# Window attention with a Sinkhorn mixture of experts on one core: the order of filler products, of the first weights' preparation and of two small copies

## Chip, cores and metric

The kernel runs on one core of one Trainium2 chip. The metric is the device time of one execution in microseconds (us), from the first to the last instruction and a little around it. Four compute engines and the DMA queues each work through their own list of instructions in order, and wait for each other by semaphores: TensorE (PE; its weight loads are PEld), VectorE (DVE), ScalarE (ACT), GpSimd (POOL), and SyncE (SP), from which all DMAs of this kernel are issued.

## What is computed

Attention over a window of 64 positions, for 4 batches of 8 heads, 576 positions and 64 columns a head, then a mixture of 8 experts over the 2304 x 512 result:

```python
def _attn_ref(q, k, v):
    scores = scale * np.matmul(q, k.transpose(0, 1, 3, 2))
    mask = (rel >= 0) & (rel < window)
    scores = np.where(mask, scores, -1000000000.0)
    scores = scores - np.max(scores, axis=-1, keepdims=True)
    attn = np.exp(scores)
    attn = attn / (np.sum(attn, axis=-1, keepdims=True) + 1e-09)
    return np.matmul(attn, v).astype(np.float32)

def _moe_ref(x, w_gate, w1, w2):
    logits = x @ w_gate
    P = np.exp(logits - logits.max())
    for _ in range(8):
        P /= P.sum(1, keepdims=True) + 1e-09
        P /= P.sum(0, keepdims=True) + 1e-09
        P *= N / E
    for e in range(E):
        out += P[:, e:e + 1] * (np.maximum(x @ w1[e], 0.0) @ w2[e])
    return out
```

with q, k, v of (4, 8, 576, 64), w_gate (512, 8), w1 (8, 512, 1024), w2 (8, 1024, 512), all float32.

## The kernel before

The 2304 rows are 18 tiles of 128. All products of the experts are made from values split in a high and a low part (three products in place of one). The program's order is written out by hand: each engine executes its instructions in the order in which the code emits them.

**Stage 1** (0 to 184 us of the trace) is the attention, a loop over steps s = 0 to 18 (the tiles, and one more). A full step emits, in this order: SP loads k and q of tile s + 2 (`load_kq`), v and the shifted v; PE makes the score products of tile s (`products`), DVE adds the mask and takes the maximum (`masked`); in even steps the gate product of an earlier pair of tiles (`gate`, ACT copies it out); PE transposes k and q of tile s + 1 (`transposes`; DVE evacuates k to kT, ACT q to qT, POOL copies the overlap of kT); ACT makes the exponentials of the first half (`exps`), DVE masks the second half; then a first `do_fill`; then PE transposes the first half of tile s - 1's weights (`attn_T`; ACT copies them to aT), DVE and POOL normalise the first half of tile s (`normalise`), PE transposes the second half of tile s - 1; ACT makes the exponentials of the second half; then a second `do_fill`; in even steps `gate_T`; then the values of tile s - 1 (`values`: PE, then the xs or xc cast and the xr copy on ACT with a DVE subtraction between them); then the second half of tile s is normalised, its DVE sum behind the subtraction of `values`. So attn_T of a step waits for normalises of the step before it, and the DVE work of each step's end comes after the values.

**Fillers.** For the six pairs of tiles that the first MoE pass does not take, the first 512 columns of expert 0 are worked out within the attention: four `mm1_s` (12 matmuls of 256 columns) and two `mm2_s` (12 of 512, whose result ACT copies and SP stores) for each pair. They wait in the list `fill`; `do_fill(n)` adds n to a credit and starts what the credit pays for, an mm1 at 0.5 and an mm2 at 1. `SHARE` gives 1 and 0.5 to the two places of steps 3 to 6 and 9 to 12, and 0.5 and 0.5 to the others. That deals: three mm1 in step 3; mm1 and mm2 in 4; mm2 and mm1 in 5; three mm1 in 6; nothing ahead of attn_T and one mm2 behind it in 7 and 8; the same again in 9 to 14; an mm1 at both places in 15 and 16; nothing ahead and an mm2 behind in 17 and 18; the last pair's six after the loop.

**Weights within stage 1.** `fetch_s` loads w1 and w2 of the fillers in two halves each; `warm_weights` splits the next half (`split_s`: ACT casts, POOL subtracts), in steps 1, 2 and twice in step 3, in step 3 once before and once behind the second `do_fill`. The first pass's weights follow: `fetch1(0)` (SP) and `sums1(0)` (four POOL operations) at the end of step 14, `split1(0)` (three ACT casts, three POOL subtractions), `fetch1(1)` and `fetch2(0)` at the end of step 15, `sums1(1)` at the end of step 17. The ring `stg` has two buffers in this stage, so `fetch2(0)` reuses the one that `split1(0)` reads. At the end of steps 6, 12 and 16 POOL also sums a pair of x (`x_sums`), whose casts (ACT) and subtractions (POOL) follow through the list `later`, one at each of two places in a step.

**First MoE pass** (184 to about 700 us). 16 units u of two weight groups each: 14 products by `Group.run`, then six `mm2(u, t)`, 12 matmuls of 512 columns each into one of two y banks. In unit 0 (expert 0, first columns) ACT copies y to acc; later units add on DVE. Between the mm2 stand Sinkhorn's steps, one at t = 0, 2, 4 (`step()` takes the next of `pending`: seven times column and row, a last column, then `prob_rows(1)` and `prob_rows(2)`), so the last column step falls in unit 2 at t = 2, `prob_rows(1)` at t = 4, `prob_rows(2)` in unit 3 at t = 0. `prob_rows` copies six rows' probabilities to `own` in three DVE copies, transposes that on PE, and stores it. DVE's sums of w2 (`sum_step`) stand between the mm2 as well, and POOL prepares the next weights.

**Second and third pass** (to the end) are not touched.

Of the kernel before, what the change touches and what calls it, by code (L numbers as in the profile page):

```python
# [8 lines left out]
F32 = mybir.dt.float32  # L9
# [12 lines left out]
def window_attention_sinkhorn_moe(ctx: ExitStack, tc: tile.TileContext, q, k, v, w_gate, w1, w2, out):  # L22
    nc = tc.nc
    B, H, S, D = q.shape
    NT, DM = out.shape
    E, _, FF = w1.shape
    P = 128
    WIN = 64
    T = NT // P
# [3 lines left out]
    ITERS = 8  # L33
    TP = 6
    NPASS = T // TP
    PAIRS = [[2, 5, 7], [1, 4, 8], [0, 3, 6]]
# [19 lines left out]
    prob = const.tile([P, T + 1, E + 1], F32, name="prob")  # L56
# [70 lines left out]
    def fetch1(i):  # L127
        if i < len(groups):
            e, c = groups[i]
            stg = r_stg.new()  # L130
            nc.sync.dma_start(out=stg, in_=w1[e, :, c * 2 * P:(c + 1) * 2 * P].rearrange("(k p) f -> p k f", p=P))
            raw1[i] = stg
# [141 lines left out]
    def mm2(u, t):  # L274
        i0 = 2 * u
        e, c = groups[i0]
        yp = ps["y"]()
        o, n = divmod(t, 2)
        o *= P
        i = 0  # L280
        for gi in (i0, i0 + 1):
            for f in range(2):
                g, w = gt_[gi, f, n], wt2[gi, f]
                for a, x in ((0, 0), (0, 1), (1, 0)):
                    nc.tensor.matmul(yp, lhsT=g[:, a, o:o + P], rhs=w[:, x, :], start=(i == 0), stop=(i == 11))  # L285
                    i += 1
        at = acc[:, t, :]
        tt = TILES[0][t]
        pr = prob[:, tt, e:e + 1]
        first = c == 0  # L290
        if e == 0:
            if first:
                nc.scalar.copy(out=at, in_=yp)  # L293
            else:
                nc.vector.tensor_tensor(out=at, in0=yp, in1=at, op=ALU.add)
        elif e == 1:

            a1 = side["acc"][:, t, :]
            if first:
                nc.scalar.copy(out=a1, in_=yp)  # L300
            else:
                nc.vector.tensor_tensor(out=a1, in0=yp, in1=a1, op=ALU.add)
        else:
            if first and e == 2:
                nc.scalar.activation(out=at, in_=at, func=AF.Copy, scale=prob[:, tt, 0:1])
                nc.vector.scalar_tensor_tensor(out=at, in0=side["acc"][:, t, :], scalar=prob[:, tt, 1:2], in1=at, op0=ALU.mult, op1=ALU.add)
            nc.vector.scalar_tensor_tensor(out=at, in0=yp, scalar=pr, in1=at, op0=ALU.mult, op1=ALU.add)  # L307
# [27 lines left out]
    with tc.manual_schedule():  # L335
        with ExitStack() as p1:
# [268 lines left out]

            fill = []

            credit = [0.0]
            SHARE = {s: (1, 0.5) if s < 15 and s % 6 in (3, 4, 5, 0) else (0.5, 0.5) for s in range(3, T + 1)}

            def do_fill(n):
                credit[0] += n
                while fill and credit[0] >= fill[0][0]:
                    cost, f = fill.pop(0)
                    f()
                    credit[0] -= cost

            new_kT(0)
            nc.vector.memset(kT[0][:, :, 0:WIN], 0.0)
# [6 lines left out]
            def warm_weights(s):  # L626
                if first and s > 0:
                    split_s(first[0][0], first[0][1], held.pop(0))
                    first.pop(0)
# [10 lines left out]
            for s in range(T + 1):  # L640
                if s + 2 < T and s != 3:
                    load_kq(s + 2)
                if s == 1:
                    held.append(fetch_s("w1", 2))
                if s < T:
                    load_vs(s)
                if s + 1 < T:
                    load_v(s + 1)
                if s == 3:
                    x_parts(0)  # L650
                if s == 0:
                    held.append(fetch_s("w1", 0))
                if s == 1:
                    nc.sync.dma_start(out=wg[:, :, 0:E], in_=w_gate.rearrange("(k p) e -> p k e", p=P))
                if s == 2:
                    held.append(fetch_s("w2", 0))
                    load_kq(5)
                    held.append(fetch_s("w2", 2))
                joint = 2 <= s < T
                ahead = s in (1, 2)  # L660
                if s < T:
                    products(s, (0, 1) if joint else (0,))
                    masked(s, 0)
                if s >= 4 and s % 2 == 0:
                    gate((s - 4) // 2)
                if s < 2:
                    keep_clock(4 if s else 0)
                if s == 3:
                    keep_clock(4, ps["h"]()[:, :P])
                    do_fill(SHARE[s][0])  # L670
                if s + 1 < T:
                    transposes(s + 1)
                if s == 1:
                    keep_clock(2)
                if s < T and not ahead:
                    exps(s, 0)
                if joint:
                    masked(s, 1)
                if later:
                    later.pop(0)()  # L680
                if s > 3:
                    do_fill(SHARE[s][0])
                if 0 <= s - 1 < T:
                    attn_T(s - 1, 0)
                if s < 2:
                    products(s, (1,))
                    masked(s, 1)
                if ahead:
                    if s == 2:
                        keep_clock(11, ps["h"]()[:, :P])  # L690
                    attn_T(s - 1, 1)
                    exps(s, 0)
                if s < T:
                    normalise(s, 0)
                if s == 0:
                    keep_clock(4)
                if 0 <= s - 1 < T and not ahead:
                    attn_T(s - 1, 1)
                if s > 2:
                    warm_weights(s)  # L700
                if s == 2:
                    values(1, lambda: exps(2, 1))
                elif s < T:
                    exps(s, 1)
                if later:
                    later.pop(0)()
                if s > 2:
                    do_fill(SHARE[s][1])
                if s == 3:
                    warm_weights(s)  # L710
                if s >= 4 and s % 2 == 0:
                    gate_T((s - 4) // 2)
                if s == 1:
                    keep_clock(4)
                if 0 <= s - 1 < T:
                    if s != 2:
                        values(s - 1)
                    raw.pop(("v", s - 2), None)
                if s < T:
                    normalise(s, 1)  # L720
                if s < 3:
                    warm_weights(s)
                if s >= 2 and s % 2 == 0:
                    j = s // 2 - 1
                    if j:
                        x_parts(j)
                    if PASS[2 * j][0]:
                        for c in range(4):
                            fill.append((0.5, lambda c=c, j=j: mm1_s(j, c)))
                        for t in (2 * j, 2 * j + 1):  # L730
                            fill.append((1, lambda t=t: mm2_s(t)))
                if s == T - 4:
                    fetch1(0)
                    sums1(0)
                if s == T - 3:
                    split1(0)
                    fetch1(1)
                    fetch2(0)
                if s == T - 1:
                    sums1(1)  # L740

            do_fill(0.5)
            gate(T // 2 - 1)
            do_fill(1)
            gate_T(T // 2 - 1)
            nc.vector.tensor_reduce(out=max1, in_=logit, axis=AX.XY, op=ALU.max)
            do_fill(1)
# [62 lines left out]
        with ExitStack() as p2:  # L810
# [12 lines left out]
            pending = []  # L823
# [24 lines left out]
            def sk_col():  # L848
# [4 lines left out]
                nc.vector.reciprocal(out=c, in_=c)  # L853
                nc.vector.tensor_tensor(out=pv, in0=pv, in1=c[:, None, :].to_broadcast([P, T, E]), op=ALU.mult)

            def prob_rows(p):
                n = TP * (E + 1)
                rp = sk_tile([n, P], "rp")
                own = sk_p.tile([P, TP, E + 1], F32, tag="own", name="own", bufs=1)
                for i, j in enumerate(PAIRS[p]):  # L860
                    nc.vector.tensor_copy(out=own[:, 2 * i:2 * i + 2, :], in_=prob[:, 2 * j:2 * j + 2, :])
                nc.tensor.transpose(rp, own.rearrange("p t e -> p (t e)"), ident)
                row = sk_p.tile([n, P], F32, tag="row", name="row")
                nc.scalar.copy(out=row, in_=rp)
                nc.sync.dma_start(out=prow[p], in_=row)

            sk_exp()
            sk_row()
            pending += [lambda: (sk_col(), sk_row())] * (ITERS - 1) + [sk_col] + [lambda p=p: prob_rows(p) for p in prow]

            for _ in range(2):
                nc.tensor.matmul(ps["b"](), lhsT=xc[0][:, 0, 0, 0:P], rhs=xc[0][:, 0, 0, :], start=True, stop=True)
# [629 lines left out]
```

## Time and profile before

| | us |
|---|---|
| median of 3 runs (lowest to highest) | 1588.26 (1586.72 to 1590.82) |
| the profiled execution, its own time | 1586.67 |
| its span, first to last instruction | 1584.9 |
| PE busy | 1553.6 (98%) |
| POOL busy | 1011.2 (64%) |
| DVE busy | 972.4 (61%) |
| ACT busy | 770.0 (49%) |

The span falls in stage 1 (184 us), the first pass (to about 700 us) and the two others. An engine's busy time leaves out what it waits. The chain of waits follows the work that ended last back from the end: at each step to what released it, or to the instruction before it on its engine; it tells which engine's time is the kernel's time. A view of a stretch gives for each engine its busy time and, in brackets, its instructions; PEclk is the clock granted to TensorE as a share of 2.4 GHz.

### The profile page before, as it was taken

The numbers are of one execution on the slowest core, as the hardware profiler recorded it, in microseconds if no ns is written. First come the engines' busy times: TensorE is split into PE (matmuls) and PEld (weight loads), VectorE is DVE, ScalarE is ACT, GpSimd is POOL, SyncE is SP. The second block draws the span as 40 slices with busy tenths as digits, with TensorE's granted clock in tenths as the row PEclk, the third lists the DMA queues.
The fourth block names the chain that finished last, engine by engine and source line by source line (L and its number), as shares of the span: only waits on it lengthen the run. The fifth ranks groups of instructions, "written<-read, shape, count | busy, mean of one in ns | idle before, by whom it ended". The sixth has DMA issues, their size and how long they took to land.

```text
span 1584.9 us, 27121 instructions
## 1 busy us (share of the span) xinstructions
PE 1553.6 (98%) x9643; PEld 1477.5 (93%) x9643; DVE 972.4 (61%) x1803; ACT 770.0 (49%) x1692; POOL 1011.2 (64%) x943
## 2 busy tenths in 40 slices
PE   8998989899999999999999999999999999999998
PEld 7786778789989988999999999999999999999998
DVE  6778257555554555555667566566656566576576
ACT  6667443444433443346455555445465454454453
POOL 6436376656785787526766766656676656657665
PEclk9999999999999999999999999999999999999999
DMA  9786355647676766697577676565885565665652
GB/s 214 176 187 156 114 199 208 211 174 259 226 285 225 260 207 243 227 328 243 184 227 239 200 249 203 189 213 177 296 305 184 183 220 177 192 221 172 198 168 100
DMA packets 235989, 334.39 MB, mean 211 GB/s; under 512 B 70818, under 2 KB 150286, under 8 KB 231886
## 3 DMA queue, kind: packets, MB, share of 16 engines
q1 hardware_dynamic: 235854, 332.66, 65.3%
q8 instruction: 76, 1.25, 0.3%
q14 instruction: 59, 0.48, 0.1%
HBM read 238.57 MB, written 90.63 MB: 208 GB/s over the span
## 4 chain that ended last, share of the span: by engine, by line
PE 93%; DVE 3%; ACT 1%; POOL 1%; DMA 1%; issue 1%; SPq 0%; ACTq 0%; POOLq 0%; DVEq 0%
PE qb L226 18%; PE y L285 15%; PE qa L226 12%; PE qc L226 12%; PE qb L1213 12%; PE qa L1213 8%; PE qc L1213 8%; PE yp L600 2%; PE hp L586 2%; PE vp L496 1%; PE tp L481 1%; DMA acc<-in_moe_w_dram 1%; PE sp L427 1%; PE tp L407 0%; DVE nm L453 0%
## 5 line engine op out<-in xcount | busy, mean ns | idle before, releaser
L226 PE MATMUL qb<-xc,w1c 128*128 128x384 f32 x1656 | 328.4, 336 | 0.0
L1100 POOL TENSOR_TENSOR G<-sm,G 128x384 fp32r<-128x384 f32 x176 | 179.0, 1017 | 195.7 <-ACT G L1096 195.7
L226 PEld LDWEIGHTS qb<-xc,w1c 128*128 128x128 f32 x1656 | 291.2, 188 | 0.7 <-ACT qb L1114 0.3
L285 PE MATMUL y<-w2c,g 128*128 128x512 f32 x1152 | 271.4, 394 | 4.5 <-ACT acc L293 4.1
L285 PEld LDWEIGHTS y<-w2c,g 128*128 128x128 f32 x1152 | 217.1, 190 | 51.1 <-ACT acc L293 4.5
L226 PE MATMUL qa<-xc,w1c 128*128 128x384 f32 x1104 | 218.2, 337 | 0.0
L226 PE MATMUL qc<-xc,w1c 128*128 128x384 f32 x1104 | 217.8, 336 | 0.0
L226 PEld LDWEIGHTS qa<-xc,w1c 128*128 128x128 f32 x1104 | 194.6, 188 | 1.2
L226 PEld LDWEIGHTS qc<-xc,w1c 128*128 128x128 f32 x1104 | 194.4, 188 | 0.0
L1221 DVE TENSOR_TENSOR acc<-qb,acc 128x384 f32<-128x384 f32 x171 | 95.0, 555 | 123.3 <-PE qb L1213 110.7
L185 POOL TENSOR_TENSOR w2c<-stg,w2c 128x512 fp32r<-128x512 f32 x64 | 89.8, 1423 | 114.5 <-PE qb L226 107.9
L794 POOL TENSOR_TENSOR w2c<-wr,w2c 128x512 fp32r<-128x512 f32 x99 | 126.5, 1297 | 34.5 <-ACT w2c L793 30.8
L794 POOL TENSOR_TENSOR wp<-wr,wp 128x512 fp32r<-128x512 f32 x100 | 127.8, 1297 | 27.5 <-ACT wp L793 22.6
L1096 ACT CAST G<-sm 128x384 fp32r<-128x384 f32 x180 | 92.3, 514 | 64.3 <-DVE sm L1107 64.3
L1213 PE MATMUL qb<-G,w2c 128*128 128x384 f32 x552 | 111.2, 336 | 0.0
L1213 PE MATMUL qb<-G,wp 128*128 128x384 f32 x528 | 106.2, 336 | 0.0
L307 DVE SCALAR_TENSOR_TENSOR acc<-y,prob,acc 128x512 f32<-128x512 f32 x72 | 54.0, 750 | 74.1 <-PE y L285 73.5
L1213 PEld LDWEIGHTS qb<-G,w2c 128*128 128x128 f32 x552 | 97.7, 188 | 0.0
L1213 PEld LDWEIGHTS qb<-G,wp 128*128 128x128 f32 x528 | 93.4, 188 | 0.0
L1221 DVE TENSOR_TENSOR acc<-qc,acc 128x384 f32<-128x384 f32 x116 | 64.3, 555 | 41.6 <-PE qc L1213 41.1
L171 POOL TENSOR_TENSOR w1c<-ws,w1c 128x1024 fp32r<-128x1024 f32 x32 | 80.4, 2512 | 0.0
L1107 POOL TENSOR_TENSOR r<-sm,r 128x384 f32<-128x384 f32 x60 | 61.0, 1017 | 30.0 <-DVE sm L1107 22.1
(217 smaller groups left out, 2850.1 us busy)
## 6 DMA issues: line engine op xcount, KB each, us to landing
w1c<-w1d SPq DMA_DIRECT2D x300, 256.0 KB, 4.4
w1d<-w1c SPq DMA_DIRECT2D x30, 1792.0 KB, 7.6
stg<-in_moe_w_dram SPq DMA_DIRECT2D x68, 512.0 KB, 4.0
w1c<-w1d SPq DMA_DIRECT2D x60, 512.0 KB, 4.8
wr<-w2d SPq DMA_DIRECT2D x114, 256.0 KB, 3.5
wr<-in_moe_w_dram SPq DMA_DIRECT2D x85, 256.0 KB, 3.9
w2d<-tf SPq DMA_DIRECT2D x30, 512.0 KB, 4.7
vs<-v SPq DMA_DIRECT2D x35, 128.0 KB, 4.3
```

The lines of the kernel that those rows point to most:

```text
L171: nc.gpsimd.tensor_tensor(out=w[:, sl, 1], in0=src.rearrange("p (s k) f -> p s k f", k=2), in1=f32(w[:, sl, 0]), op=ALU.subtract)
L185: nc.gpsimd.tensor_tensor(out=w[:, 1], in0=src[:, j], in1=f32(w[:, 0]), op=ALU.subtract)
L226: nc.tensor.matmul(bank, lhsT=w[:, ws, a, kk, :], rhs=xc[xs][:, b, kk, :], start=(first and j == 0), stop=(j == 5), skip_group_check=not f ...
L285: nc.tensor.matmul(yp, lhsT=g[:, a, o:o + P], rhs=w[:, x, :], start=(i == 0), stop=(i == 11))
L307: nc.vector.scalar_tensor_tensor(out=at, in0=yp, scalar=pr, in1=at, op0=ALU.mult, op1=ALU.add)
L586: nc.tensor.matmul(hp, lhsT=w1s[c][:, a, kk, :], rhs=xs[j][:, b, kk, :], start=(i == 0), stop=(i == 3 * KD - 1))
L794: nc.gpsimd.tensor_tensor(out=t[:, :, 1, :], in0=r, in1=f32(t[:, :, 0, :]), op=ALU.subtract)
L1096: nc.scalar.copy(out=self.g[:, k, 0, :], in_=src)
L1100: eng.tensor_tensor(out=self.g[:, k, 1, :], in0=src, in1=f32(self.g[:, k, 0, :]), op=ALU.subtract)
L1107: eng.tensor_tensor(out=dst, in0=x, in1=y, op=op)
L1213: nc.tensor.matmul(bank, lhsT=W[p, u, wp][:, g, y, cols], rhs=G7[p, 2 * u + g][:, gp, x, :], start=(start and j == 0), stop=(j == 5), skip ...
L1221: nc.vector.tensor_tensor(out=at, in0=src, in1=at, op=ALU.add)
```

## The change

- In unit 0 the copy of y to acc goes from ACT to DVE.
- `do_fill(n)` takes n fillers, whatever they cost: one ahead of attn_T from step 3 on, one behind it in steps 3 to 16, none behind it in 17 and 18. That deals two mm1 to steps 3, 4, 6, 7, 9, 10, 12, 13, 15 and 16, two mm2 to steps 5, 8, 11 and 14, and one mm2 ahead of attn_T to 17 and 18; after the loop the order is as before.
- The second call of `warm_weights` in step 3 is gone; the last half (w2) is split by the call in step 4, ahead of the second `do_fill`.
- `fetch1(0)` goes from the end of step 14 to that of 7, `sums1(0)` from 14 to 8, `split1(0)` with `fetch1(1)` and `fetch2(0)` from 15 to 11, `sums1(1)` from 17 to 14.
- The three DVE copies to `own` for each of passes 1 and 2 are made right after the last column step, into two buffers; `prob_rows` only transposes, copies and stores.

```diff
         if e == 0:
             if first:
-                nc.scalar.copy(out=at, in_=yp)
+                nc.vector.tensor_copy(out=at, in_=yp)
...
-            credit = [0.0]
-            SHARE = {s: (1, 0.5) if s < 15 and s % 6 in (3, 4, 5, 0) else (0.5, 0.5) for s in range(3, T + 1)}
-
             def do_fill(n):
-                credit[0] += n
-                while fill and credit[0] >= fill[0][0]:
-                    cost, f = fill.pop(0)
+                for f in fill[:n]:
                     f()
-                    credit[0] -= cost
+                del fill[:n]
...
                 if s == 3:
                     keep_clock(4, ps["h"]()[:, :P])
-                    do_fill(SHARE[s][0])
+                    do_fill(1)
...
                 if s > 3:
-                    do_fill(SHARE[s][0])
+                    do_fill(1)
...
-                if s > 2:
-                    do_fill(SHARE[s][1])
-                if s == 3:
-                    warm_weights(s)
+                if 2 < s < T - 1:
+                    do_fill(1)
...
-                            fill.append((0.5, lambda c=c, j=j: mm1_s(j, c)))
+                            fill.append(lambda c=c, j=j: mm1_s(j, c))
                         for t in (2 * j, 2 * j + 1):
-                            fill.append((1, lambda t=t: mm2_s(t)))
-                if s == T - 4:
+                            fill.append(lambda t=t: mm2_s(t))
+                if s == 7:
                     fetch1(0)
+                if s == 8:
                     sums1(0)
-                if s == T - 3:
+                if s == 11:
                     split1(0)
                     fetch1(1)
                     fetch2(0)
-                if s == T - 1:
+                if s == 14:
                     sums1(1)
 
-            do_fill(0.5)
+            do_fill(1)
             gate(T // 2 - 1)
-            do_fill(1)
+            do_fill(2)
...
+            own_rows = {}
+
+            def gather(p):
+                own_rows[p] = own = sk_p.tile([P, TP, E + 1], F32, tag="own", name="own")
+                for i, j in enumerate(PAIRS[p]):
+                    nc.vector.tensor_copy(out=own[:, 2 * i:2 * i + 2, :], in_=prob[:, 2 * j:2 * j + 2, :])
+
             def prob_rows(p):
...
-                own = sk_p.tile([P, TP, E + 1], F32, tag="own", name="own", bufs=1)
-                for i, j in enumerate(PAIRS[p]):
-                    nc.vector.tensor_copy(out=own[:, 2 * i:2 * i + 2, :], in_=prob[:, 2 * j:2 * j + 2, :])
+                own = own_rows.pop(p)
...
-            pending += [lambda: (sk_col(), sk_row())] * (ITERS - 1) + [sk_col] + [lambda p=p: prob_rows(p) for p in prow]
+            pending += [lambda: (sk_col(), sk_row())] * (ITERS - 1) + [lambda: (sk_col(), [gather(p) for p in prow])] + [lambda p=p: prob_rows(p) for p in prow]
```

## Rows read from the trace of the kernel before

**Rows 1.** The page's part 4: chain that ended last, share of the span by engine.
```profile
PE 93%; DVE 3%; ACT 1%; POOL 1%; DMA 1%; issue 1%; SPq 0%; ACTq 0%; POOLq 0%; DVEq 0%
```

**Rows 2.** Waits of PE, 0 to 184 us: for whom, us in total, times, longest.
```profile
PE tp L481 <- POOL s L475: 8.2, 4, 2.9
```

**Rows 3.** Waits of PE, 184 us to the end.
```profile
PE qc L862 <- DVE own L861: 4.2, 2, 3.6
PE y L285 <- ACT acc L293: 4.1, 1, 4.1
```

**Rows 4.** Busy time by stretch, columns as headed; steps 4, 7, 9, 12, 15, 16.
```profile
core 0: us, PE busy (x) PEld busy (x) DVE busy (x) ACT busy (x) POOL busy (x), PEclk, DMA share, GB/s
33.73:47.32 13.59, 10.80 (x119) 8.75 (x115) 6.80 (x15) 8.14 (x22) 7.78 (x8) 0.87 0.71 159
64.61:73.01 8.40, 7.15 (x96) 5.72 (x92) 6.02 (x12) 6.43 (x19) 5.71 (x7) 1.00 0.46 93
...
82.12:90.42 8.30, 8.30 (x121) 7.93 (x117) 6.83 (x15) 5.71 (x17) 2.80 (x4) 1.00 0.82 200
107.72:116.96 9.24, 9.24 (x130) 8.24 (x126) 7.02 (x17) 6.28 (x19) 2.48 (x3) 1.00 0.94 213
...
134.48:142.03 7.55, 7.05 (x108) 6.47 (x104) 6.08 (x14) 5.44 (x16) 1.72 (x3) 1.00 0.77 221
142.03:150.84 8.81, 8.04 (x119) 6.83 (x115) 8.25 (x14) 7.43 (x21) 8.73 (x10) 1.00 0.71 148
```

**Rows 5.** Busy time by stretch: the six mm2 of units 0, 3, 5.
```profile
199.07:222.30 23.23, 19.11 (x79) 15.36 (x79) 12.07 (x25) 9.31 (x17) 21.07 (x19) 0.93 0.48 160
...
301.92:323.53 21.61, 18.00 (x74) 14.44 (x74) 10.80 (x16) 4.77 (x9) 12.61 (x11) 0.92 0.51 170
369.81:386.20 16.39, 16.39 (x74) 13.55 (x74) 9.33 (x13) 4.03 (x8) 16.08 (x18) 1.00 0.48 174
```

**Rows 6.** Busy time by stretch: five us in step 18.
```profile
165.00:170.00 5.00, 5.00 (x44) 3.84 (x43) 0.23 (x1) 0.62 (x2) 4.20 (x7) 0.71 0.01 2
```

**Rows 7.** PE in order of time, steps 10 and 11: start, us, what, idle before.
```profile
92.87 1.68 PE L586 MATMUL hp<-xs,w1s 128*128 128x256 f32 x12
94.38 1.15 PE L481 MATMUL tp<-ident,s 128*128 128x128 f32 x8
95.29 2.99 PE L600 MATMUL yp<-w2c,g 128*128 128x512 f32 x12
98.12 0.38 PE L552 MATMUL hp<-ident,gt 128*128 128x128 f32 x2
...
99.51 1.10 PE L427 MATMUL sp<-kT,qT 64*64 64x128 f32 x32
100.55 1.09 PE L407 MATMUL tp<-ident,kq 128*128 128x128 f32 x8
```

**Rows 8.** ACT in order of time, end of step 3: cast of w2's second half.
```profile
36.47 1.14 ACT L578 CAST w2c<-acc 128x512 fp32r<-128x512 f32 x2 [1.57 <-DMA acc<-in_moe_w_dram]
```

**Rows 9.** POOL in order of time, step 15: first of the four sums.
```profile
141.91 0.73 POOL L151 TENSOR_TENSOR ws<-stg 128x256 f32<-128x256 f32 x1 [3.81 <-DMA stg<-in_moe_w_dram]
```

**Rows 10.** Waits of the DMA queue (SP), 130 to 160 us.
```profile
SPq L141 <- POOL w1c L171: 5.3, 1, 5.3
```

**Rows 11.** DMA issues: times, KB each, median us from issue to landing.
```profile
kq<-in_q_dram SPq DMA_DIRECT2D x15, 256.0 KB, 5.4
```

**Rows 12.** ACT in order of time, step 17.
```profile
155.31 0.40 ACT L465 ACTIVATE s<-s,nm 128x128 f32<-128x128 f32 x1 [1.80 <-DVE nm L453]
...
156.86 0.77 ACT L532 CAST xc<-xt 128x256 fp32r<-128x256 f32 x2
157.54 1.07 ACT L483 COPY aT<-tp 128x512 f32<-128x512 f32 x2
```

**Rows 13.** ACT in order of time, unit 0.
```profile
206.54 1.04 ACT L169 CAST w1c<-ws 128x1024 fp32r<-128x1024 f32 x1 [4.32 <-POOL ws L154]
```

**Rows 14.** Line 861's instructions: count, duration in ns min/median/max, starts.
```profile
L861 DVE COPY own<-prob x6: 160/164/2366, 281.8 to 308.2; 128x18 f32<-128x18 f32 x6
```

## The prediction

> **What bounds the kernel now.** I read the chain of waits first: TensorE (PE) holds 93% of it [rows 1]. So a term counts only if it shortens PE's row, and every other engine matters by when it releases PE. Next I read whom PE waited for, before and after 184 us [rows 2, 3]: the waits sit in the attention (stage 1, steps s = 0 to 18) and in the first units of the first MoE pass; after 345 us hardly any is left. A wait costs more than its idle time. In the 5 us behind the wait at 160 us the granted clock averages 0.71 [rows 6]: part of them ran at 1.2 in place of 2.4 GHz, which costs 5 x 0.29 = 1.45 us.
>
> Then the length of each step, between the starts of the score products [rows 4], against its pieces. Start to start, an mm1 filler takes 94.38 - 92.87 = 1.51 us and an mm2 filler 98.12 - 95.29 = 2.83 us [rows 7]. Step 9 (three mm1, PE never idle) lasts 8.30, so a bare odd step is 8.30 - 4.53 = 3.77 us; step 12 gives 9.24 - 4.53 = 4.71 us for an even one (it has gate and gate_T). What a step lasts beyond bare + fillers is its loss:
> - step 4: 13.59 - (4.71 + 1.51 + 2.83) = 4.5 us;
> - step 7, which has no filler ahead of attn_T: 8.40 - (3.77 + 2.83) = 1.8 us. Steps 8, 13 and 14 repeat it; the even ones idle 0.1 us less, so I take 4 x 1.7 = 6.8 us;
> - step 15: 7.55 - 6.79 = 0.76 us; step 16: 8.81 - 7.73 = 1.1 us;
> - steps 17 and 18: of four waits for POOL, 8.2 us in all [rows 2], 2.8 belong to step 4, which leaves 5.4. Step 7 loses 1.8 for two waits in which PE idles 8.40 - 7.15 = 1.25 us [rows 4], so each wait also costs some 0.25 of drained pipeline: 5.4 + 0.75 + 1.45 for the clock = 7.6 us.
>
> **The change part by part.** The fillers themselves are the same 36, so only losses change.
>
> *w2's second half split in step 4.* In step 3 ACT waited 1.57 us for the DMA of that half and then copied it ahead of the xs cast [rows 8]; DVE's softmax sum, POOL's normalise and the second attn_T of step 4 came late by that. Moved behind attn_T in step 4, the copy finds its data landed, and step 4 now needs no mm2 (its fillers are the last two mm1), so nobody needs these weights before step 5. What is late next is the first w2 half, which ACT reaches 1.5 us earlier; left over 0.4 us (0 to 1.5). Gain 4.1 us.
>
> *Two fillers to each step, one of them ahead of attn_T.* Steps 7, 8, 13, 14 get their cover. In 8 and 14 it is an mm2 of 2.83 us, more than the loss: nothing is left. With an mm1 of 1.51 us in an odd step the nearest row is step 15, which has just this deal: 0.76 us. Steps 7 and 9 then lose 0.8 and 0.75 us (step 9 lost nothing before, with two mm1 ahead), steps 6, 10 and 16 0.1 to 0.2 each, step 3 0.1. Apart from 13, that is 6.8 - 2.2 = 4.6 us, between 3.0 and 6.8.
>
> *Weights of the pass: fetch in step 7, sums in 8, split at the end of 11, second sums in 14.* It ends the loss of steps 16 to 18 (1.1 + 7.6 = 8.7), in which POOL's normalises were late behind the weights' work. The sums (four operations of 0.73 us, which before first stood 3.81 us for their DMA [rows 9]) now meet landed data in steps 9 and 15 and end before their results or the next kT copy are due; I take 0, up to 0.7 each. The split moves whole, and with it its DMAs. Three ACT copies (2 us) again stand before qT of step 12; step 16 lost 1.1 us with the same copies, so 1.1 here. Behind them the fetch into the first stg buffer must wait till POOL has read it: the DMA queue on SyncE stood 5.3 us there [rows 10]. Before, no k and q load was behind it (step 16 has none). Now that of tile 14 is. POOL should be free for the split some 1.5 us sooner after the step's start than before, so the queue reopens about 6 us into step 12, and k and q issue there at 6.2 and 6.9 us. Landing takes 5.4 us for q in the median [rows 11], so q is there at some 12.3 us, while PE, after a step of 8.8 us and 1.0 us of products, wants k at 9.8 and q at 10.2. Loss in step 13: 2.1 us (0.5 with a landing of 4 us, 5 with POOL as late as before); the POOL and DVE backlog is under it. So of 8.7 us, 3.2 come back at 12 and 13.
>
> *Steps 17 and 18 as dealt now.* mm2 stands ahead of attn_T in both, and covers the wait for POOL (2.83 against 2.9, 0.3 left in 18). But in 17 nothing follows attn_T: PE runs straight into the values, whose aT copies stand on ACT behind four exponentials (155.31 to 156.86), two casts (0.68) and the mm2 copy [rows 12]. Products (1.04 us, from 99.51 to 100.55 [rows 7]) and mm2 end 3.9 us into the step, the two transposes at 4.7; ACT starts its exponentials at some 3.2 and gives the first aT at 3.2 + 1.55 + 0.7 + 0.5 + 0.6 = 6.6. Loss 2.0 us (0 if ACT is earlier, 3.5 with the clock). Stage 1 in sum: 4.1 + 4.6 + 8.7 - 3.2 - 2.0 - 0.3 = 11.9 us.
>
> *First copy of unit 0 on DVE.* y of the third tile waited 4.1 us for an ACT copy [rows 3], because ACT sat 4.32 us on POOL's ws [rows 13] with the copies behind it. The six products last 23.23 us there against 16.39 in a steady unit [rows 5], and three small Sinkhorn products lie between: loss 6.3. DVE has nothing due then but the Sinkhorn steps (3 us each, three of them) and one sum of w2 for each tile from the third on. Two tiles last 5.7 us of PE; DVE's share in that time is two copies of 0.7, about 3 us of Sinkhorn and two sums of 0.4 to 1.5: 5.2 to 7.4. So DVE runs close behind. I take 0.7 left, gain 5.6 (3.0 to 6.3).
>
> *Rows gathered a step earlier.* PE waited 4.2 us for `own` in units 2 and 3, the longer time 3.6 [rows 3]; unit 3 lasts 21.61 - 16.39 = 5.2 us over, clock included. Gathered with the last column step, in unit 2, the second row is ready long before: gain 4.9. For the first row 0.6 is to be had (0 to 0.7): of six copies five or so take 0.16 us and one stood 2.37 us [rows 14]; at six after the column step that is 3.2 us, done 1 us before the transposition. The Trainium skill (SBUF — State Buffer, "Who interferes with whom") explains that row by a port pair that VectorE's copies and GpSimd share and of which one holder blocks the other for a whole instruction. Were each copy to meet another POOL operation, the first row would be 0.3 to 0.6 us late, and the sum 0.6 us smaller; the row shows one such wait for three copies.
>
> **The sum.** 11.9 + 5.6 + 4.9 + 0.6 = 23.0 us. The profiled execution took 1586.67 us (span 1584.9), so 1563.7; it lies 1.6 us below the median of the runs, 1588.26, for which I say 1565.3.
>
> **Rivals.**
> - *The loads of tile 14 are later still:* POOL is as late as before, the loss in 13 is 5 us, and the clock falls behind a wait that long (1.45): 1565.3 + 4.4 = 1569.7. For it: the queue row. Against it: POOL's lateness there began with the sums that stood for their DMA [rows 9].
> - *DVE takes ACT's place in unit 0:* the third or sixth product waits for a DVE copy that queues behind Sinkhorn and sums, and the 5.6 us are not gained: 1570.9. For it: DVE's 5.2 to 7.4 against 5.7. Against it: two y banks, and a queue that is empty at the start.
> - *The deal covers nothing,* because attn_T waits for work that starts only at the end of the values, and what an odd step spares the next loses; stage 1 gains nothing: 1577.2. Against it: in steps 9 and 12 PE was never idle [rows 4].
> - *Slower:* one filler ahead of attn_T leaves a short idle time in most of the steps 6 to 17, and TensorE is granted 1.2 GHz through them. A stretch at that level costs half its length, so from 46 us of the stage's 184 on the gain is gone; with 60 us at it the time is 1565.3 + 30 = 1595. Against it: step 7, idle for 1.25 us, shows 1.00 throughout [rows 4]; the clock fell behind waits of 2.8 us and more.
>
> **How the numbers follow.** Forecast 0.58, late loads 0.20, DVE 0.09, nothing covered 0.04; same (within 0.3%, some 4.8 us, about what a measurement tells from no change) 0.05; slower 0.04. The bounds of the terms give gains of 9 to 30 us; the ends don't meet, and 13 to 29 hold the forecast and the first two rivals: 1559 to 1575.5. Faster 0.91, same 0.05, slower 0.04.
>
> **What will show it.** Steps 7, 8 and 14 without a wait of attn_T over 0.5 us; no wait on POOL in 4, 17 and 18; a new wait of PE for k or q in step 13 and for aT in 17; unit 0 at about 17.5 us and unit 3 at 16.6, at clock 1.00. I am wrong if unit 0 keeps over 20 us with a DVE copy as the releaser, or if steps 12 and 13 last over 21 us together.

## The result, and the profile after

The changed kernel takes 1565.36 us (median of 4 runs, 1565.21 to 1567.77) against 1587.99 us for the kernel before: a ratio of 0.9859, 95% interval 0.9842 to 0.9876. The forecast was 1565.3. The profiled execution took 1565.21 us with a span of 1563.4; the sum had given 1563.7 for it. So it misses 1.5 us of the 23.0 of the sum. The median is met by luck: this execution lies 0.15 us below the median of its runs, where the one of before lay 1.6 us below.

Whom PE waits for in the changed kernel, first up to 172 us (stage 1), then to the end: us in total, times, longest. They answer to [rows 2, 3].

```profile
PE vp L496 <- ACT aT L483: 2.8, 4, 1.7
PE tp L481 <- DVE kT L409: 2.1, 4, 0.6
PE tp L407 <- DMA kq<-in_k_dram: 1.9, 1, 1.9
PE tp L407 <- DMA kq<-in_q_dram: 1.4, 2, 0.8
```

```profile
PE qb L226 <- ACT qb L246: 1.1, 1, 1.1
```

The 8.2 us for POOL's normalises, the 4.2 for `own` and the 4.1 for ACT's copy are gone. So are the four waits of attn_T for ACT's qT in steps 7, 8, 13 and 14, which stood in the same view of before as

```profile
PE tp L481 <- ACT qT L411: 3.1, 4, 0.8
```

In their place stand waits for k and q (step 13), for aT (1.7 us of it in step 17), and one that was not forecast, for ACT's copy of qa in unit 6.

The stretches that answer to [rows 4, 5]: steps 4, 5, 7, 13 and 17, then the six mm2 of units 0 and 3, and the products of unit 6's first group. Columns: stretch, length, PE busy (instructions), granted clock, DMA share, GB/s.

```profile
32.06:40.40 8.34, 7.95 (x118) 1.00 1.05 248
40.40:50.79 10.39, 9.76 (x108) 1.00 1.16 258
58.70:66.27 7.57, 7.15 (x108) 1.00 0.93 220
109.78:119.53 9.75, 7.08 (x108) 1.00 1.05 220
145.31:153.11 7.80, 6.07 (x88) 1.00 0.25 70
188.21:205.59 17.38, 17.38 (x80) 1.00 0.27 81
284.68:301.19 16.51, 16.51 (x75) 1.00 0.53 194
363.66:379.64 15.98, 14.87 (x85) 1.00 0.98 348
```

Step 4 fell from 13.59 to 8.34 us (1.3 of it because it now has two mm1 and no mm2), unit 0's mm2 from 23.23 to 17.38, unit 3's from 21.61 to 16.51, all at clock 1.00. From stretch to stretch: stage 1 ends 10.9 us earlier (the first product of unit 0 starts at 173.64, not 184.51), unit 0 gives 5.85, unit 2 0.8, unit 3 5.1, unit 8 0.8; units 1 and 6 cost 0.25 and 1.4. That adds up to 21.8 us; the span is shorter by 21.5.

### The profile page after: what moved, and what is told of

It is laid out like the page before. It is cut to its first block, busy times and chain, and to the rows that moved or that the text cites. A ratio compares the mean times of both kernels' runs of the same rounds, so it can differ in the third digit from the quotient of the medians.

```text
span 1563.4 us, 27128 instructions
## 1 busy us (share of the span) xinstructions
PE 1546.5 (99%) x9643; PEld 1473.8 (94%) x9643; DVE 973.3 (62%) x1809; ACT 764.5 (49%) x1686; POOL 1014.7 (65%) x943
## 4 chain that ended last, share of the span: by engine, by line
PE 92%; DVE 2%; ACT 2%; POOL 2%; DMA 1%; issue 1%; SPq 0%; POOLq 0%; ACTq 0%; DVEq 0%
PE qb L226 18%; PE y L285 15%; PE qb L1212 12%; PE qa L226 12%; PE qc L226 12%; PE qc L1212 8%; PE qa L1212 8%; PE yp L600 2%; PE hp L586 1%; PE vp L496 1%; PE tp L481 1%; DMA tf<-xd_f 1%; POOL w1c L171 1%; PE sp L427 1%; DMA kq<-in_q_dram 1%
## 5 line engine op out<-in xcount | busy, mean ns | idle before, releaser
L285 PE MATMUL y<-w2c,g 128*128 128x512 f32 x1152 | 267.7, 391 | 0.2 <-DVE acc L307 0.2
L169 ACT CAST w1c<-ws 128x1024 fp32r<-128x1024 f32 x32 | 33.7, 1054 | 111.3 <-POOL ws L154 111.3
```

What stands on the lines that cost most here:

```text
L169: nc.scalar.copy(out=w[:, sl, 0], in_=src.rearrange("p (s k) f -> p s k f", k=2))
```

## The experiments

All but two are edits of the changed kernel; the two are that kernel and the kernel before, run once more. A ratio is to runs of the kernel before on the same chip; one more set of runs of the unchanged changed kernel (below) gave 1566.35 us and 0.9866 (0.9851 to 0.9881), so 0.9859 to 0.9866 is what they are held against. With intervals of some 0.0016 to either side, a difference of 2 or 3 us can't be read from the ratios; there the traces are read. This table gives, from the starts of the score products in each trace, how long parts of stage 1 take (us; a step is counted from its score products to the next, the last column from step 17 to the first product of unit 0):

| kernel | steps 3 to 5 | 6 to 11 | 12 | 13 | 14 | 16 | 17 to end |
|---|---|---|---|---|---|---|---|
| before | 31.57 | 52.19 | 9.24 | 8.41 | 9.11 | 8.81 | 33.67 |
| before, again | 29.58 | 52.17 | 9.37 | 8.39 | 9.11 | 8.56 | 33.71 |
| changed | 27.11 | 50.63 | 8.36 | 9.75 | 10.31 | 7.91 | 28.33 |
| changed, again | 27.10 | 50.65 | 8.34 | 11.11 | 10.30 | 7.91 | 28.33 |
| w2 split in 3 | 30.46 | 50.63 | 8.34 | 9.96 | 10.31 | 7.91 | 28.31 |
| weights late | 27.15 | 50.63 | 7.90 | 7.57 | 10.31 | 8.49 | 28.72 |
| dealt as before | 31.45 | 52.13 | 10.43 | 8.86 | 9.11 | 7.91 | 30.98 |
| fetch later | 27.11 | 50.63 | 8.34 | 8.75 | 10.31 | 7.90 | 28.33 |
| step 17's casts moved | 27.15 | 50.64 | 8.34 | 12.92 | 10.28 | 7.90 | 27.17 |
| three mends | 27.17 | 50.62 | 7.91 | 7.58 | 10.32 | 8.52 | 28.25 |

Step 15 takes 7.55 or 7.56 us in all of them.

**Unit 0's copy on ACT again.**

```diff
-                nc.vector.tensor_copy(out=at, in_=yp)
+                nc.scalar.copy(out=at, in_=yp)
```

> The changed kernel with one part undone: in unit 0 ACT copies y to acc again. Theory (the term of the prediction): the copies stand behind ACT's wait for POOL's ws again, the third product waits some 4.1 us for its bank and the clock falls behind it; the six products of unit 0 last 23.2 us and not 17.4, the whole is 5.6 us slower than the changed kernel, about 1571. Rival: what freed unit 0 is the earlier work on the weights (second sums in step 14), not the engine of the copy; then unit 0 stays under 18 us and the time within 1 us of 1565.4.

Measured: 1573.31 us, ratio 0.9922 (0.9905 to 0.9938). Unit 0's six mm2 by stretch, and PE's waits from 172 to 300 us:

```profile
188.30:212.76 24.46, 20.35 (x79) 0.86 0.46 161
```

```profile
PE y L285 <- ACT acc L293: 4.1, 1, 4.1
```

The same single wait of 4.1 us as in [rows 3] is back, and the six mm2 take 7.1 us more than on DVE. It is more than the 5.6 expected because the clock granted in the stretch is 0.86 here, where it was 0.93 in [rows 5]: the wait is the same, what the clock adds behind it isn't. DVE, on the other hand, leaves nothing: PE is busy for all of its 17.38 us.

**Rows gathered as late as before.**

```diff
 def prob_rows(p):
+    gather(p)
-... + [lambda: (sk_col(), [gather(p) for p in prow])] + ...
+... + [sk_col] + ...
```

> The changed kernel with one part undone: the own rows are gathered in prob_rows again, one buffer. Theory: PE waits 3.6 us for own in unit 3 and 0.6 us in unit 2, the clock falls in unit 3; unit 3 lasts 21.6 us and not 16.5, unit 2 17.9 and not 17.2; 5.8 us slower than the changed kernel, about 1571. Rival: DVE comes to unit 3 earlier than before, because other waits ahead of it are gone, and meets POOL idle; then unit 3 stays under 18 us and the time within 2 us of 1565.4.

Measured: 1572.04 us, ratio 0.9909 (0.9894 to 0.9923). PE's waits from 172 to 330 us, and the six mm2 of units 2 and 3:

```profile
PE qc L862 <- DVE own L855: 4.2, 2, 3.6
```

```profile
253.37:271.35 17.98, 17.36 (x79) 1.00 0.47 175
285.94:307.83 21.89, 18.28 (x75) 0.92 0.50 169
```

The waits of [rows 3] return to the tenth, with 0.8 us in unit 2 (17.19 changed) and 5.4 in unit 3: 6.2 us, against 5.5 in the sum.

**w2's second half split in step 3 again.**

```diff
+                if s == 3:
+                    warm_weights(s)      # behind the second do_fill, as before
```

> The changed kernel with one part undone: the second half of the fillers' w2 is split in step 3 again, behind the second filler. Theory: ACT waits for that DMA ahead of the xs cast, as before (1.57 us, and now from an earlier start, so some 3 us); the second attn_T of step 4 waits 2.8 us or more for POOL and the clock falls: step 4 lasts 12.5 to 13 us and not 8.3, step 5 gets back the 0.9 us that the moved casts cost it there; 3 to 4 us slower, about 1569. Rival: the dealing, which took the mm2 out of step 4, had already made the split harmless; then within 1 us of 1565.4.

Measured: 1568.14 us, ratio 0.9886 (0.9871 to 0.9900). Steps 4 and 5 by stretch, with all engines, and PE's wait between 25 and 55 us:

```profile
32.20:44.82 12.62, 9.37 (x118) 8.15 (x114) 7.13 (x16) 7.86 (x22) 8.16 (x8) 0.86 0.98 233
44.82:54.31 9.49, 9.49 (x108) 7.96 (x104) 5.74 (x12) 5.97 (x16) 2.48 (x3) 1.00 0.90 199
```

```profile
PE tp L481 <- POOL s L475: 3.2, 1, 3.2
```

Step 4 takes 4.3 us more, with the wait for POOL and the low clock; step 5 takes 0.9 less, without a wait. Both halves of the move are thus seen: 4.3 gained in step 4, 0.9 lost in step 5.

**The weights of the first pass at their old place, the new deal kept.**

```diff
-                if s == 7:
+                if s == T - 4:
                     fetch1(0)
-                if s == 8:
                     sums1(0)
-                if s == 11:
+                if s == T - 3:
                     split1(0)
                     fetch1(1)
                     fetch2(0)
-                if s == 14:
+                if s == T - 1:
                     sums1(1)
```

> The changed kernel with one part undone: fetch, sums and split of the pass's first weights at the ends of steps 14, 14, 15 and 17 again; the fillers dealt as in the changed kernel. Theory (the prediction's terms): the move was worth 8.7 - 3.2 = 5.5 us, so steps 16 to 18 lose as before and the time is about 1571. Rival: the dealing alone (an mm2 ahead of attn_T in 17 and 18) covers POOL's lateness there; step 13 gets back 2.3 to 3 us and step 12 0.5 us, step 16 loses 1 us and step 17 some 1 us more; then the time is within 1.5 us of 1565.4, on either side.

Measured: 1563.98 us, ratio 0.9852 (0.9837 to 0.9866). Not slower at all. PE's waits up to 172 us, the longest line and the one for POOL:

```profile
PE vp L496 <- ACT aT L483: 3.7, 5, 2.2
...
PE tp L481 <- POOL s L475: 0.2, 1, 0.2
```

With the weights as late as before, POOL costs PE 0.2 us, where [rows 2] show 8.2. Of these, 2.8 stood in step 4, where this kernel keeps the moved w2 split; the 5.4 of steps 17 and 18 were ended by the deal.

**The old deal, with w2's old split, the weights early.**

```diff
+            credit = [0.0]
+            SHARE = {s: (1, 0.5) if s < 15 and s % 6 in (3, 4, 5, 0) else (0.5, 0.5) ...}
...
-                    do_fill(1)
+                    do_fill(SHARE[s][0])
```

> The changed kernel with the dealing of before (credits), and with it the split of w2's second half in step 3, which that dealing needs; weights, copy and gathering stay as changed. Theory: step 4 loses 4.5 us again, steps 7, 8 and 14 1.8, 1.6 and 1.6, step 18 3 us and the clock; steps 9, 12 and 5 get back 0.8, 0.4 and 0.9: 10 to 12 us slower than the changed kernel, about 1576. Rival: what idles in 7, 8 and 14 is only moved by the dealing (attn_T waits for work that begins at the end of the values): then 3 to 5 us slower, for step 4, about 1569.

Measured: 1575.55 us, ratio 0.9925 (0.9910 to 0.9939). PE's waits up to 182 us, and PE in order of time around attn_T of steps 17 and 18:

```profile
PE tp L481 <- POOL s L475: 7.1, 3, 2.9
```

```profile
154.87 0.65 PE L481 MATMUL tp<-ident,s 128*128 128x128 f32 x4 [1.53 <-POOL s L475]
155.28 3.01 PE L600 MATMUL yp<-w2c,g 128*128 128x512 f32 x12
...
163.42 0.66 PE L481 MATMUL tp<-ident,s 128*128 128x128 f32 x4 [2.89 <-POOL s L475]
```

The weights' work lies steps earlier, and attn_T of step 17 and 18 still waits 1.53 and 2.89 us for POOL, 4.4 of the 5.4 us of before: nothing stands ahead of it, and the filler comes behind the wait.

Together with the kernel before and the last experiment this makes a square. The time from step 6 to the end of stage 1 (the table's columns and step 15, which the w2 split doesn't touch; the new deal has one mm1 more there, whose 1.51 us are taken off):

| us | weights late | weights early |
|---|---|---|
| old deal | 128.99 | 126.97 |
| new deal | 119.67 | 121.34 |

The deal alone gives 9.3 us, the weights alone 2.0, both 7.65. On top of the new deal the early weights cost 1.7 (they gain 0.6 in step 16 and 0.4 from 17 on, and cost 0.5 in 12 and 2.2 in 13), and 1.4 more where the clock falls in step 13, as in the changed kernel's second profile.

**`fetch2(0)` two steps later.** It was to tell whether the queue behind the stg buffer makes the wait in step 13.

```diff
                     fetch1(1)
-                    fetch2(0)
+                if s == 13:
+                    fetch2(0)
```

> The changed kernel with fetch2(0) at the end of step 13 in place of step 11, so that the loads of k and q of tile 14 are not queued behind its wait for POOL. Theory: PE's wait for k and q in step 13 (1.86 and 0.81 us) goes, step 13 lasts 7.5 us like step 15 and not 9.75: 2.2 us faster, about 1563. Rival: POOL, with the split's three operations, and DVE behind it are late by about as much, which the DMA's wait hides now; then attn_T of step 13 waits for POOL or DVE and the gain is under 0.8 us.

Measured: 1564.10 us, ratio 0.9863 (0.9848 to 0.9878). PE's waits between 100 and 125 us, first of the changed kernel, then of this one:

```profile
PE tp L407 <- DMA kq<-in_k_dram: 1.9, 1, 1.9
PE tp L407 <- DMA kq<-in_q_dram: 0.8, 1, 0.8
PE tp L481 <- DVE kT L409: 0.5, 1, 0.5
```

```profile
PE tp L481 <- DVE kT L409: 1.7, 2, 1.2
PE vp L496 <- ACT aT L483: 0.4, 1, 0.4
```

Both waits for the loads go, so the queue was their cause; behind them DVE's kT copy is late by 1.2 us, and step 13 gives back 1.0 of the 2.2 us, between what theory and rival had.

**Step 17's casts and mm2 copy moved out of aT's way.**

```diff
-                if later:
+                if later and s != T - 1:
                     later.pop(0)()
...
+            while later:
+                later.pop(0)()
             do_fill(1)
...
-(nc.vector.tensor_copy if j == T // 2 - 1 else nc.scalar.copy)(out=ys, in_=yp)
+(nc.vector.tensor_copy if j == T // 2 - 1 or t == 12 else nc.scalar.copy)(out=ys, in_=yp)
```

> The changed kernel with ACT relieved in step 17: no casts of x sums ahead of attn_T there (they come one place later, the last ones after the loop), and the mm2 result of that step copied on DVE. Theory: PE's wait for aT in step 17 (1.73 us) is ACT's queue: four exponentials, two casts (0.7), the copy (0.5), aT; without the two the wait falls by 1.2 us to 0.5, about 1564.2. Rival: the exponentials alone, or DVE's maximum ahead of them, set aT, or step 18 waits longer for POOL instead: gain under 0.4 us.

Measured: 1563.86 us (1562.69 to 1569.51), ratio 0.9849 (0.9832 to 0.9865). The wait for aT falls from 1.73 us to

```profile
PE vp L496 <- ACT aT L483: 0.6, 1, 0.6
```

and the end of stage 1 takes 27.17 us for 28.33. In its profiled execution, the longest of its runs, step 13 lasts 12.92 us. It stands here in four stretches, and below as one stretch in the changed kernel's second profile and in that of the second pass's sums behind the products (both experiments follow):

```profile
111.00:113.50 2.50, 0.69 (x28) 1.00 1.24 255
113.50:117.00 3.50, 2.32 (x10) 0.59 0.85 182
117.00:120.00 3.00, 3.00 (x16) 0.50 1.11 212
120.00:124.00 4.00, 4.00 (x67) 0.88 1.14 190
```

```profile
109.98:121.09 11.11, 8.46 (x109) 0.85 1.25 227
```

```profile
109.98:122.69 12.71, 9.88 (x109) 0.73 1.13 212
```

Behind the waits for k and q TensorE was granted 1.2 GHz (0.50) in some executions, and 2.4 (1.00) in others.

**The changed kernel again.**

> The changed kernel once more, unchanged, to see what repeats. Theory: PE's wait of 1.1 us for ACT in unit 6 hangs on the landing of one DMA (the sums of the third pass's x, 9.6 us from issue to landing against 7.8 before, where 0.5 us was left), so with another landing it is between 0 and 1.5 us; the waits of stage 1 (k and q in 13, aT in 17) repeat within 0.3 us. Rival: the wait in unit 6 belongs to the changed order and repeats as 1.1 us.

Measured: 1566.35 us, ratio 0.9866 (0.9851 to 0.9881). Every step but 13 takes what it took in the first profile, to 0.05 us; step 13 takes 1.4 more, at clock 0.85, and unit 6's products 16.50 for 15.98.

**The second pass's sums behind the products.** It is about unit 6. Its first ACT copy comes late, because ACT's cast ahead of it waits for POOL, and POOL for a load. POOL and ACT of the changed kernel in order of time:

```profile
348.91 0.73 POOL L314 TENSOR_TENSOR xt<-tf 128x256 f32<-128x256 f32 x1 [7.88 <-DMA tf<-xd_f]
```

```profile
365.57 1.05 ACT L169 CAST w1c<-ws 128x1024 fp32r<-128x1024 f32 x1 [8.65 <-POOL ws L154]
366.52 0.47 ACT L246 COPY qb<-qa 128x384 f32<-128x384 f32 x1
```

```diff
-                next_sums(2, u - 5)                    # even(3): DMA and four POOL sums
+                todo.append(next_sums(2, u - 5))       # even(3): DMA alone
...
+                    elif k == 3 and todo:              # odd(3): the sums
+                        todo.pop()()
```

> Part of the changed kernel's remainder: from unit 5 on the four sums of the second pass's x (on POOL) are issued behind the products of the unit's second group, not right behind their DMA. In every profile of the changed kernel and its variants PE waits 0.6 to 2.0 us in unit 6 for ACT's copy of qa, ACT for POOL's ws, and POOL stands some 8 us for the DMA tf<-xd_f. Theory: with the sums behind that DMA moved back, ws is early, unit 6 and 7 take 14.59 us for their first group again, and the time is 1.1 to 2.2 us less than the changed kernel's: some 1563.7. Rival: POOL is then late with the low halves of w1, the wait moves to a later product of unit 6, and the time stays at 1565 to 1566.

Measured: 1565.15 us, ratio 0.9867 (0.9850 to 0.9883). PE's only wait from 176 to 700 us and POOL's for the load:

```profile
PE y L285 <- DVE acc L307: 0.2, 1, 0.2
```

```profile
POOL xt L314 <- DMA tf<-xd_f: 1.3, 1, 1.3
```

Units 6 and 7 take 14.59 us for their first group again, though the load took 10.1 us, so the mechanism holds. The time doesn't show it: in the profiled execution (1567.19 us) step 13 cost 12.7 us, and that spread of step 13 is larger than what unit 6 gives.

**w2's casts behind the xs cast.**

```diff
-                if s > 2:
+                if s == 3:
                     warm_weights(s)
...
                         values(s - 1)
+                    if s == 4:
+                        warm_weights(s)
```

> The changed kernel with the split of w2's second half in step 4 moved from behind attn_T to behind the values (two ACT copies and two POOL subtractions). Theory: step 5 lost 0.96 us because these two ACT copies stood ahead of the xs cast; with them behind it step 5 falls from 10.39 to some 9.4 us and the time by 1.0 us: 1564.4. Rival: the first mm2 of step 5 then waits for these weights, step 5 stays at 10 us or more, and nothing is gained.

Measured: 1566.18 us, ratio 0.9875 (0.9860 to 0.9889). The rival held: step 5 takes 10.67 us, for 10.39. PE's wait for kT there (0.63 us) is gone, as the theory had it, but the mm2 now waits for the weights:

```profile
PE yp L600 <- POOL w2c L579: 0.5, 2, 0.3
```

So in step 5 the two casts are late for the one or the other; with the split back in step 3 (above) it took 9.49 us without a wait.

**The kernel before once more.**

> The kernel before once more, for a second profile of it. If the landing of tf<-xd_f in unit 5 varies from execution to execution, it should take 9 to 10 us here at times too and unit 6 be longer than 14.59; if it is the change that made it slower, it takes some 7.8 us again (7.82 in the first profile, 8.6 to 10.2 in the nine of the changed kernel and its variants) and unit 6 has no wait. Likelier: the second, as nine of nine lie above. Step 4 at 13.6, unit 0's six products at 23.2 and unit 3's at 21.6 again.

Measured: 1588.93 us. The likelier case was wrong: tf<-xd_f took 9.97 us here, and units 6 and 7 wait, as unit 6 does in the changed kernel. Step 4, unit 0's and unit 3's mm2, unit 6's products by stretch, then PE's wait for POOL in step 4 and, of its waits behind 184 us, the one that [rows 3] don't have:

```profile
34.10:45.70 11.60, 9.47 (x119) 1.00 0.68 159
```

```profile
197.32:221.84 24.52, 20.41 (x80) 0.86 0.45 161
301.44:323.34 21.90, 18.29 (x75) 0.92 0.51 170
385.82:402.05 16.23, 14.87 (x86) 1.00 0.97 344
```

```profile
40.79 0.66 PE L481 MATMUL tp<-ident,s 128*128 128x128 f32 x4 [2.13 <-POOL s L475]
```

```profile
PE qb L226 <- ACT qb L246: 2.0, 2, 1.4
```

The wait of unit 6 is therefore no cost of the change: the kernel before has it too, in one of its two profiles. Step 4 takes 11.60 us at clock 1.00, where [rows 4] have 13.59 at 0.87. Of the 2.0 us, 0.7 are the wait for POOL, which lasted 2.13 us here and 2.79 there, and 1.3 are PE's busy time (9.47 for 10.80), so the clock.

**Three mends together**: the weights late, step 17's casts moved, the sums behind the products.

> The changed kernel with the weights of the pass back at their old place (steps 15, 16 and 18), step 17's later copies behind the values, and the second pass's x sums behind the second group's products. Theory: the steps of e4 (12 at 7.9, 13 at 7.6, 16 at 8.5), step 17 some 1.2 us shorter as in e7, unit 6 at 14.59: 1563.98 of e4 less 1.2 less 1.6 to 1.9, so 1561 (1560 to 1562.5). Rival: behind the late weights ACT's aT in step 17 stays late, or the wait in unit 6 only moves: 1563 to 1564.

Measured: 1562.23 us (1561.31 to 1562.40), ratio 0.9849 (0.9835 to 0.9864), span 1560.0. All its runs lie below all runs of the two variants on the same chip, the sums behind the products and the w2 casts behind the xs cast (1564.17 to 1567.49). They lie below all eight of the changed kernel too (1563.73 to 1568.33 in the second set, 1565.21 to 1567.77 in the first), but the kernel before took 1586.18 us on this chip and 1588.33 on that of the second set, and the intervals of the ratios overlap. By the traces step 13 takes 7.58 us and unit 6 has no wait. Step 17's mend gave 0.5 us here (28.25 for the 28.72 of the weights late alone), not 1.2: PE still waits 1.66 us for aT. ACT begins its exponentials there 4.5 us into the step (at 147.87, step 17 starting at 143.40), because DVE's maximum is late:

```profile
147.87 0.40 ACT L465 ACTIVATE s<-s,nm 128x128 f32<-128x128 f32 x1 [1.79 <-DVE nm L453]
```

With the weights late it is not the casts alone that hold aT; why the maximum is later here stays open.

## Why the prediction was right, and where it was right for the wrong reason

**The total** (23.0 us forecast, 21.8 found stretch by stretch) holds within its range, and so does the sum for stage 1 (11.9 against 10.9). Part of that is luck: terms that were missed (step 5, unit 6, and unit 8 the other way) cancel in part. And two of its terms are wrongly divided. *Where it failed:* "It ends the loss of steps 16 to 18 (1.1 + 7.6 = 8.7), in which POOL's normalises were late behind the weights' work." The waits for POOL in 17 and 18 were there because no filler stood ahead of attn_T, exactly what the prediction says of step 7; early weights alone left 4.4 of the 5.4 us. For steps 6 to the end it counted 5.5 for the weights and 2.3 for the deal (4.6 less 2.0 and 0.3); the square shows 9.3 for the deal, and the weights cost 1.7 on top of it. The two errors are one, an effect put down to the wrong one of two edits that act on the same waits, so the sum (7.8 against 7.65) didn't suffer; that it came out is no proof of the shares.

**w2's split.** The gain in step 4 is right against the profile it was read from (3.9 us beyond the lighter fillers, for 4.1; 4.3 when undone). Against the second profile of before, with its shorter wait and clock 1.00, it is 1.9. What failed is "what is late next is the first w2 half": late next were the moved copies themselves, on ACT ahead of the xs cast that ends step 4's work; DVE's kT copy for step 5 comes behind it. That 0.96 us of step 5 (10.39 less 3.77 and two mm2) is in no term.

**Steps 7, 8, 9, 14.** 7 and 9 keep 0.8 each (7.57 and 7.56 for 6.79), 8 and 14 nothing beyond a pair of mm2 (10.3 for 10.37), as forecast. The short idle times leave the clock at 1.00 there, so the slower rival's mechanism doesn't act in them; and the square's 9.3 us rule out the rival in which the deal covers nothing.

**Steps 12 and 13.** 12 lost 0.63 us (forecast 1.1). In 13 both loads were awaited where the prediction had them, but the term was too small: beyond its bare length and two mm1 (6.79 us) step 13 lost 2.96 us for the 2.1 forecast. Against the kernel with late weights, which loses 0.8 there without any load, it is 2.2. The time at which q landed was nearly met (12.6 us after the start of step 12, for 12.3) by two errors that cancel: q was issued 8.1 us into the step, not 6.9, and landed after 4.54 us, not 5.4. Step 12 was 0.4 us shorter than forecast, so PE stood waiting earlier. In 3 of the 8 profiles with this order the clock fell behind it and the step lasted 11.1 to 12.9 us. That is the first rival (5 us and the clock) in part: not because POOL was later, but through the clock alone.

**Step 17.** ACT began its exponentials 3.4 us into the step and gave aT at 6.6 (3.2 and 6.6 forecast); mending it gave 1.2 of the 2.0 us.

**Unit 0.** 5.85 for 5.6. The loss of 6.3 was oversized: PE is busy for all of the 17.38 us, which is 1.0 over a steady unit, and the prediction had left 0.5 for Sinkhorn's products. But DVE left nothing of the 0.7, so the two sizes make up for each other. The DVE rival is out: PE never waits for that copy.

**Rows gathered earlier.** 5.1 and 0.8 us for 4.9 and 0.6. The six copies took 4.3 us, more than the 3.2 assumed. Their durations as in [rows 14]; then the longest one on DVE, POOL's subtraction beside it, and PE's transposition of the first row:

```profile
L855 DVE COPY own<-prob x6: 163/442/2381, 263.1 to 267.3; 128x18 f32<-128x18 f32 x6
```

```profile
264.97 2.38 DVE L855 COPY own<-prob 128x18 f32<-128x18 f32 x1
264.91 2.41 POOL L171 TENSOR_TENSOR w1c<-ws,w1c 128x1024 fp32r<-128x1024 f32 x1
267.21 0.27 PE L861 MATMUL qc<-ident,own 128*54 128x128 f32 x1
```

The longest copy lasted 2.38 us beside an operation of 2.41; two more took 1.15 and 0.72, and each of the three ended within 0.04 us of the end of a subtraction on POOL. That agrees with the rule of the Trainium skill (SBUF — State Buffer, "Who interferes with whom") that a GpSimd instruction can hold VectorE's copy off for its whole length. The sum didn't pay the 1.1 us because the first row needs the first three copies alone, and these were done at 264.98, 2.2 us ahead of the transposition. The prediction had all six stand ahead of it; the sixth ended at 267.44, behind it.

**Not in the sum:** unit 6's 1.4 us. It was read as nothing because the one profile of before happened to show none; the second has it. Unit 8's 0.8 us are in no term either; both profiles of before have them and none of the changed kernel. The prediction's range, at 1559 to 1575.5, holds all sets of runs of the changed kernel.

What stays open: why the clock falls behind step 13 in some executions and not in others with waits as long, and why the load of tf takes 7.8 us in one execution and 10 in another of the same kernel. Neither was tried further. Open too is what took 0.8 us in unit 8 of the kernel before; 0.2 of it is a wait of PE for ACT.

## What to carry to other kernels

Where two edits of one change act on the same wait, cost them as a square (neither, one, the other, both) and give the shared gain to the one that acts at the place of the wait; an edit that gains alone may cost on top of the other, and leaving it out may be the better kernel. A copy that is moved behind a wait is still an instruction on its engine: look who stands behind it in the new place, in the next step too. One profile of before is one execution: a margin of half a microsecond, as ACT's in unit 6 (0.48 us idle ahead of its copy of qa), is no proof that nothing waits there.

## What was not expected of the hardware

- After waits of nearly the same length in step 13 (2.6 to 3.0 us in all for k and q) the granted clock was 1.00 throughout in one execution of the changed kernel (9.75 us for the step), 0.85 over the step in another (11.11), and 0.50 for some 6 us in the variant with step 17's casts moved (12.92). The length of the wait doesn't decide it alone: the clock stayed at 1.00 behind 2.87 us, with w2 split in 3, and fell behind 2.64, in the changed kernel's second execution. Likewise behind unit 0's 4.1 us on ACT: 0.93 or 0.86 over the stretch, 23.23 or 24.5 us.
- The same load of 512 KB (tf<-xd_f in unit 5), issued at the same place of the program, landed after 7.82 us in one execution of the kernel before and after 9.97 in another; in the variants it took 8.6 to 10.2.
